# Attention and two mixture layers: the block-diagonal query tile written by ScalarE instead of copied by DMA

## Chip, cores and metric

The kernel runs on one core of a Trainium2 chip. A core has TensorE (PE in the profile; its weight loads are PEld), VectorE (DVE), ScalarE (ACT), GpSimd (POOL) and SyncE (SP, which issues the DMAs). The metric is the device time of one execution in microseconds; lower is better.

## The reference

Three steps follow each other; the change is in the first.

- Attention: q, k, v have shape (4, 8, 1152, 64), float32. Two neighbouring queries are averaged, which leaves 576 per head; then softmax(q_pool k^T / 8) v, with the row maximum subtracted before the exponential and 1e-9 added to the sum.
- A mixture of 8 experts over the 2304 tokens of 512 features: tokens are assigned greedily by sorted logits with a capacity of 288 each, then relu(x w1) w2.
- A dense layer: g = h - tanh(h) with h = x w_in, then g w_out.

## The kernel before, in words

Heads are handled two at a time, 16 pairs P = 0 to 15. The loop in `run` does the scores, exponentials and products with v of pair P; in between, a generator `prep(P + 1)` prepares the next pair. How far it advances is written out by hand: `SCHED` lists the steps (a step is half a score tile or a place behind pv) at which the generator is resumed, "B0" while pair 0 is worked on and "B" after that. Steps 2, 2 do the two query groups, 5, 5, 6 the three key groups, and the row-maximum matmuls begin at step 8 under "B" and at step 17 under "B0". In between stand the score matmuls (L227, L228) and their exponentials (E, L229) of the pair at work, and behind step 12 the pv matmuls (L245). Each engine works its instructions in the order written.

`prep` works in float32r, a rounded float32. For the queries: three transposes on TensorE put 288 columns of both heads into a PSUM buffer "aux" (L149; rows 0 to 63 are one head, 64 to 127 the other); ScalarE rounds it into qh (L152); VectorE stores the rest, ql = ps - qh (L153). The keys go the same way in three groups of 384 columns: L169, kh on ScalarE (L172), kl on VectorE (L173).

qz is a block-diagonal tile [128, 2, 576]: half s holds head s's rows of qh in that head's partitions, and zeros, set once at the start, in the other 64. It is the stationary operand of the row-maximum matmuls (L208): 9 blocks of 128 queries by 3 groups of 384 keys, each reduced on VectorE to a column of pm (L212). There is one qz for all pairs. In pair 0, VectorE and GpSimd fill it with casts from qh (L156); in the other 15 pairs two DMAs SBUF to SBUF do (L161), issued from SyncE's queue ahead of the six copies into q1 and q2 (L163 to L165). All these DMAs are shown under line 143, where the helper `copy` stands.

There are three PSUM buffers "aux". In a pair they are taken in turn by the two query groups, the three key groups and then the L208 products, and each comes free when VectorE has read it (ql, kl or pm). The score tiles have three buffers "sc" of their own. A product with v (`pv`) ends a pair; a copy oT on ScalarE (L252) starts the next. `finish(P)` does the row sums, normalisation and router logits of pair P during pair P + 1; at its very end, for the last pair, ScalarE reads one part of an aux buffer (L288) while VectorE reduces the rest of it (L290).

Of the kernel before, what the change touches and what calls it, by code (L numbers as in the profile page):

```python
# [14 lines left out]
AF = mybir.ActivationFunctionType  # L15
# [30 lines left out]
def as32(ap):  # L46
    return ap.bitcast(F32)


class Attention:  # L50
# [78 lines left out]
    def prep(self, P):  # L129
        nc, t = self.nc, self.t[P]  # L130
        first = P == 0
        bank = "sc" if first else "aux"
        qs, kr, qz = t["qs"], t["kr"], self.qz
        ql = self.wk.tile([128, SQ], F32R, name="ql", bufs=1)
        kh = self.wk.tile([128, S], F32R, name="kh", bufs=1)
        kl = self.wk.tile([128, S], F32R, name="kl", bufs=1)
        q1 = t["q1"] = self.wk.tile([128, 2, SQ], F32R, name="q1")
        q2 = t["q2"] = self.q2[P % 2]
        k1 = t["k1"] = [self.wk.tile([128, S], F32R, name=f"k1{s}") for s in range(2)]
        k2 = t["k2"] = [self.k2[2 * (P % 2) + s] for s in range(2)]  # L140
        own = [slice(0, 64), slice(64, 128)]
        oth = own[::-1]
        copy = lambda dst, src: nc.sync.dma_start(as32(dst), as32(src))

        qh = self.wk.tile([128, SQ], F32R, name="qh", bufs=1)
        for g in range(2):
            ps = self.psum.tile([128, 3, QP], F32, name="aux", bufs=3)
            for j in range(3):
                nc.tensor.transpose(ps[:, j], qs[:, 3 * g + j].rearrange("p s d -> p (s d)"), self.ident[:QP, :QP])  # L149
            ps = ps.rearrange("p a b -> p (a b)")  # L150
            c = slice(g * HALF, g * HALF + HALF)
            nc.scalar.activation(qh[:, c], ps, AF.Copy)  # L152
            nc.vector.tensor_sub(ql[:, c], ps, as32(qh[:, c]))  # L153
            if first:
                for s, e in ((0, nc.vector), (1, nc.gpsimd)):
                    e.tensor_copy(qz[own[s], s, c], qh[own[s], c])  # L156
                self.warm(4)
            yield
        if not first:
            for s in range(2):  # L160
                copy(qz[own[s], s], qh[own[s]])  # L161
        for s in range(2):
            copy(q1[own[s], s], qh[own[s]])  # L163
            copy(q1[oth[s], s], qh[own[s]])
            copy(q2[own[s], s], ql[own[s]])  # L165
        for g in range(3):
            ps = self.psum.tile([128, 3, 128], F32, name=bank, bufs=3)
            for j in range(3):
                nc.tensor.transpose(ps[:, j], kr[:, 3 * g + j].rearrange("p s d -> p (s d)"), self.ident)  # L169
            ps = ps.rearrange("p a b -> p (a b)")  # L170
            c = slice(g * 384, g * 384 + 384)
            nc.scalar.activation(kh[:, c], ps, AF.Copy)  # L172
            nc.vector.tensor_sub(kl[:, c], ps, as32(kh[:, c]))  # L173
            if first:
                self.warm(4)
            yield
        for s in range(2):
            copy(k1[s][own[s]], kh[own[s]])
            copy(k1[s][oth[s]], kl[own[s]])
            copy(k2[s][own[s]], kh[own[s]])  # L180
        qz = qz.rearrange("p s n -> p (s n)")
        pm = self.wk.tile([128, QB, 3], F32, name="pm")
        nm = self.wk.tile([128, QB], F32R, name="nm")

        def most(s):

            nb = slice(5 * s, 5 + 4 * s)
            nc.vector.tensor_reduce(nm[:, nb], pm[:, nb], axis=AX.X, op=OP.max, negate=True)
            yield
            yield  # L190
            at = 0
            for bs in ((range(4), range(4, 5)), (range(4, 5), range(5, 9)))[s]:
                ps = self.psum.tile([128, 512], F32, name="aux", bufs=3)
                n = 0
                for b in bs:
                    c = slice(0, 128) if b != 4 else own[s]
                    w = c.stop - c.start
                    nc.tensor.matmul(ps[:1, n:n + w], nm[:, b:b + 1], self.identr[:, c], start=True, stop=True)
                    n += w
                o = oth[s].start  # L200
                nc.scalar.activation(q2[o:o + 1, s, at:at + n], ps[:1, :n], AF.Copy)
                at += n
            yield

        for blk in range(QB):
            for pc in range(3):
                ps = self.psum.tile([128, 384], F32, name="aux", bufs=3)
                nc.tensor.matmul(ps, qz[:, blk * 128:blk * 128 + 128], kh[:, pc * 384:pc * 384 + 384],  # L208
                                 start=True, stop=True)
                if first and blk < 5:  # L210
                    self.warm(4)
                nc.vector.tensor_reduce(pm[:, blk, pc:pc + 1], ps, axis=AX.X, op=OP.max)  # L212
                yield
            if blk == 4:
                yield from most(0)
                if first:
                    yield "head"
        yield from most(1)
# [1073 lines left out]
```

## Time and profile before

| | |
|---|---|
| median of 3 runs | 1366.21 us (1364.76 to 1367.0) |
| the profiled execution | 1365.93 us |
| its span in the profile | 1364.1 us |
| TensorE busy | 1238.7 us (91%) |
| VectorE busy | 1050.1 us (77%) |
| ScalarE busy | 709.4 us (52%) |
| GpSimd busy | 571.2 us (42%) |

Times inside the profile are microseconds from the start of the span. A busy engine is not by itself a bound: what counts is which engine the others waited for at each place. The attention part covers about the first 600 us; a pair takes about 36 us.

### The profile page before, as it was taken

How to read it: one execution, taken by the hardware profiler on the slowest of the kernel's cores; microseconds unless marked ns; L12 is line 12 of the kernel's file. 1: busy time of each engine (PE TensorE's matmuls, PEld its weight loads, DVE VectorE, ACT ScalarE, POOL GpSimd, SP SyncE). 2: the span in 40 equal slices, each digit the busy share in tenths (PEclk: the TensorE clock that was granted, in tenths of full speed). 3: DMA queues.
4: the chain of work that ended last, by engine and by line, in shares of the span. 5: the costliest groups of instructions: out<-in, count | busy, mean ns of one | idle time of the engine just before them, and what ended most of it. 6: DMA issues, size and time to landing. Idle time of an engine off the chain costs nothing.

```text
span 1364.1 us, 26747 instructions
## 1 busy us (share of the span) xinstructions
PE 1238.7 (91%) x9539; PEld 1074.3 (79%) x9539; DVE 1050.1 (77%) x2384; ACT 709.4 (52%) x1892; POOL 571.2 (42%) x501
## 2 busy tenths in 40 slices
PE   7898888888988988866989999999999999999997
PEld 6666666666666666645879989899999999999997
DVE  6788888788878888886797888787877877557563
ACT  3554555555555555521455464653754645657464
POOL 5777777677667776520031221221312212222122
PEclk9999999999999999987999999999999999999999
DMA  8878878877777777325942402203114022040300
GB/s 195 217 199 207 210 205 206 209 185 180 189 204 195 202 198 195 120 67 161 323 135 72 120 17 74 79 9 101 51 33 120 17 88 65 17 135 18 95 1 18
DMA packets 164965, 175.01 MB, mean 128 GB/s; under 512 B 66400, under 2 KB 117600, under 8 KB 164832
## 3 DMA queue, kind: packets, MB, share of 16 engines
q1 hardware_dynamic: 161760, 163.86, 44.5%
q0 software_dynamic: 3072, 9.44, 2.4%
q8 instruction: 75, 1.23, 0.4%
q14 instruction: 58, 0.48, 0.1%
HBM read 100.16 MB, written 26.21 MB: 93 GB/s over the span
## 4 chain that ended last, share of the span: by engine, by line
PE 58%; DVE 29%; ACT 5%; DMA 3%; issue 3%; SPq 1%; POOL 1%; DVEq 0%; ACTq 0%; POOLq 0%
PE acc L908 19%; PE h L908 17%; PE pv L245 9%; DVE pm L212 8%; PE aux L208 4%; DVE db L789 3%; DMA qz<-qh 2%; DVE z L979 2%; PE sc L227 2%; DVE z L978 2%; DVE z L977 2%; PE sc L228 1%; DVE sm L290 1%; DVE sm L296 1%; PE aux L507 1%
## 5 line engine op out<-in xcount | busy, mean ns | idle before, releaser
L237 POOL TENSOR_TENSOR acc<-acc,E 128x576 f32<-128x576 f32 x217 | 327.3, 1522 | 106.2 <-ACT E L229 103.9
L229 ACT ACTIVATE E<-sc 128x288 f32<-128x288 f32 x576 | 224.9, 424 | 201.9 <-PE sc L228 119.7
L976 POOL TENSOR_TENSOR th<-hc,th 128x288 f32<-128x288 f32 x128 | 110.7, 865 | 383.2 <-ACT th L973 358.9
L212 DVE TENSOR_REDUCE pm<-aux 128x1 f32<-128x384 f32 x432 | 218.4, 548 | 50.1 <-PE aux L208 49.6
L908 PE MATMUL h<-yh,wi 128*128 128x288 f32 x1024 | 223.9, 300 | 3.5 <-ACT th L973 3.5
L208 PE MATMUL aux<-kh,qz 128*128 128x384 f32 x432 | 161.1, 383 | 31.5 <-DMA qz<-qh 8.9
L227 PE MATMUL sc<-q,k 128*128 128x288 f32 x576 | 183.1, 324 | 2.6 <-ACT E L229 2.3
L908 PEld LDWEIGHTS h<-yh,wi 128*128 128x128 f32 x1024 | 169.9, 189 | 5.1 <-ACT th L973 4.4
L228 PE MATMUL sc<-q,k 128*128 128x288 f32 x576 | 167.3, 295 | 0.0
L908 PE MATMUL acc<-ah,wo 128*128 128x288 f32 x1024 | 164.2, 299 | 0.0
L245 PE MATMUL pv<-E,vr 128*64 128x288 f32 x1152 | 154.0, 412 | 0.0
L908 PE MATMUL h<-yl,wi 128*128 128x288 f32 x512 | 147.4, 296 | 0.0
L908 PEld LDWEIGHTS acc<-ah,wo 128*128 128x128 f32 x1024 | 143.4, 188 | 3.1 <-issue 1.6
L208 PEld LDWEIGHTS aux<-kh,qz 128*128 128x128 f32 x432 | 79.4, 187 | 73.1 <-DVE pm L212 23.1
L227 PEld LDWEIGHTS sc<-q,k 128*128 128x128 f32 x576 | 109.2, 190 | 17.1 <-issue 8.3
L245 PEld LDWEIGHTS pv<-E,vr 128*64 128x64 f32 x1152 | 76.9, 136 | 56.1 <-issue 11.4
L977 DVE SCALAR_TENSOR_TENSOR z<-hc,z 128x288 f32<-128x288 f32 x128 | 63.5, 496 | 67.0 <-ACT mk L975 67.0
L228 PEld LDWEIGHTS sc<-q,k 128*128 128x128 f32 x576 | 109.3, 190 | 0.0
L971 ACT ACTIVATE z<-h 128x288 f32<-128x288 f32 x128 | 51.8, 405 | 89.7 <-PE h L908 89.6
L908 PEld LDWEIGHTS h<-yl,wi 128*128 128x128 f32 x512 | 95.4, 189 | 0.0
L908 PE MATMUL acc<-al,wo 128*128 128x288 f32 x512 | 88.9, 295 | 0.0
L979 DVE COPY_PREDICATED z<-mk,th 128x288 f32<-128x288 int16 x128 | 73.8, 576 | 13.6 <-DVE z L978 0.5
(246 smaller groups left out, 2481.6 us busy)
## 6 DMA issues: line engine op xcount, KB each, us to landing
k<-kh SPq DMA_DIRECT2D x64, 288.0 KB, 5.4
w1r<-in_moe_w_dram SPq DMA_DIRECT2D x64, 256.0 KB, 2.9
w2r<-in_moe_w_dram SPq DMA_DIRECT2D x64, 256.0 KB, 2.8
q<-qh SPq DMA_DIRECT2D x64, 144.0 KB, 2.6
k<-kl SPq DMA_DIRECT2D x32, 288.0 KB, 4.0
vr<-in_v_dram SPq DMA_DIRECT2D x16, 576.0 KB, 6.3
qr<-in_q_dram SPq DMA_DIRECT2D x30, 288.0 KB, 5.5
kr<-in_k_dram SPq DMA_DIRECT2D x30, 288.0 KB, 5.7
```

The costliest lines, as they stand in the source:

```text
L208: nc.tensor.matmul(ps, qz[:, blk * 128:blk * 128 + 128], kh[:, pc * 384:pc * 384 + 384], start=True, stop=True)
L212: nc.vector.tensor_reduce(pm[:, blk, pc:pc + 1], ps, axis=AX.X, op=OP.max)
L227: nc.tensor.matmul(ps, t["k1"][s][:, ks], t["q1"][:, s, qs], start=True, stop=False)
L228: nc.tensor.matmul(ps, t["k2"][s][:, ks], t["q2"][:, s, qs], start=False, stop=True)
L229: nc.scalar.activation(e[:, hf], ps, AF.Exp, scale=1.0 / 16.0)
L237: eng.tensor_add(a, a, e)
L245: nc.tensor.matmul(t["pv"][64 * s:64 * s + 64, hf, :HALF], t["vr"][:, s, c, :], t["E", c, s][:, hf], start=(c == 0), stop=(c == KC - 1), s ...
L908: self.nc.tensor.matmul(out, wl if p == 2 else wh, xl if p == 1 else xh, start=first and not seen[j], stop=last and seen[j] == 2)
L971: nc.scalar.activation(z, ps, AF.Square)
L976: nc.gpsimd.tensor_sub(th, h, th)
L977: nc.vector.scalar_tensor_tensor(z, h, LEAD, z, op0=OP.mult, op1=OP.mult)
L979: nc.vector.copy_predicated(z, mk.bitcast(mybir.dt.int16), th)
```

## The change

In `prep`, for every pair, ScalarE writes both halves of qz straight from the PSUM buffer, group by group, right behind qh and ahead of VectorE's subtraction in the program. The casts of the first pair and the two DMA copies of the other pairs go.

```diff
             nc.scalar.activation(qh[:, c], ps, AF.Copy)
+            for s in range(2):
+                nc.scalar.activation(qz[own[s], s, c], ps[own[s]], AF.Copy)
             nc.vector.tensor_sub(ql[:, c], ps, as32(qh[:, c]))
             if first:
-                for s, e in ((0, nc.vector), (1, nc.gpsimd)):
-                    e.tensor_copy(qz[own[s], s, c], qh[own[s], c])
                 self.warm(4)
             yield
-        if not first:
-            for s in range(2):
-                copy(qz[own[s], s], qh[own[s]])
```

## Rows read from the trace of the kernel before

**Rows 1.** Chain that ended last, shares of the span by line (page, part 4).

```profile
PE acc L908 19%; PE h L908 17%; PE pv L245 9%; DVE pm L212 8%; PE aux L208 4%; DVE db L789 3%; DMA qz<-qh 2%; DVE z L979 2%; PE sc L227 2%; DVE z L978 2%; DVE z L977 2%; PE sc L228 1%; DVE sm L290 1%; DVE sm L296 1%; PE aux L507 1%
```

**Rows 2.** Waits, 62 to 560 us: who <- whom: us in total, times, longest.

```profile
DVE kl L173 <- ACT kh L172: 10.8, 14, 0.8
...
PE aux L208 <- DMA qz<-qh: 8.9, 12, 1.3
...
PE aux L208 <- DVE kl L173: 1.6, 2, 1.1
```

**Rows 3.** Timeline, ScalarE, from 136 us: start us, us, instruction, [idle before].

```profile
136.33 0.74 ACT L152 ACTIVATE qh<-aux 128x288 fp32r<-128x288 f32 x2
136.91 1.06 ACT L229 ACTIVATE E<-sc 128x288 f32<-128x288 f32 x3
137.78 0.96 ACT L172 ACTIVATE kh<-aux 128x384 fp32r<-128x384 f32 x2
...
138.81 0.62 ACT L172 ACTIVATE kh<-aux 128x384 fp32r<-128x384 f32 x1
```

**Rows 4.** Timeline, VectorE, the same pair: first kl, all three, then pm.

```profile
138.39 0.56 DVE L173 TENSOR_TENSOR kl<-aux,kh 128x384 fp32r<-128x384 f32 x1 [0.78 <-ACT kh L172]
...
138.39 1.63 DVE L173 TENSOR_TENSOR kl<-aux,kh 128x384 fp32r<-128x384 f32 x3 [0.78 <-ACT kh L172]
140.04 2.42 DVE L212 TENSOR_REDUCE pm<-aux 128x1 f32<-128x384 f32 x5
...
144.27 0.56 DVE L212 TENSOR_REDUCE pm<-aux 128x1 f32<-128x384 f32 x1 [1.81 <-PE aux L208]
```

**Rows 5.** Timeline, TensorE, the same pair: L208, pv, a later L208.

```profile
139.59 0.41 PE L208 MATMUL aux<-kh,qz 128*128 128x384 f32 x1 [0.59 <-DMA qz<-qh]
...
140.99 0.33 PE L208 MATMUL aux<-kh,qz 128*128 128x384 f32 x1
...
141.43 0.34 PE L208 MATMUL aux<-kh,qz 128*128 128x384 f32 x1
141.69 0.71 PE L245 MATMUL pv<-E,vr 128*64 128x288 f32 x4
...
144.95 0.37 PE L208 MATMUL aux<-kh,qz 128*128 128x384 f32 x1
```

**Rows 6.** The copy in that pair: in the chain; in SyncE's timeline.

```profile
137.09 2.37 DMA qz<-qh
...
137.09 1.16 SPq L143 DMA_DIRECT2D qz<-qh  x2
```

**Rows 7.** ScalarE's groups by form, 62 to 560 us: busy us, mean ns, idle before.

```profile
L797 ACT ACTIVATE dh<-du 128x512 fp32r<-128x512 f32 x27 | 16.8, 622 | 17.6 <-DVE du L793 17.6
L201 ACT ACTIVATE q<-aux 1x512 fp32r<-1x512 f32 x28 | 16.4, 586 | 9.3 <-PE aux L198 9.3
```

**Rows 8.** Timelines at 598 us: two engines on one aux buffer.

```profile
598.59 0.19 ACT L288 ACTIVATION_READ_ACCUMULATOR xr<-aux 128x1 f32 x1
...
598.82 0.56 DVE L290 TENSOR_REDUCE sm<-aux 128x3 f32<-128x384 f32 x1
```

**Rows 9.** Pair 0's casts (min/median/max ns); pair 1's qs and its reader.

```profile
L156 DVE CAST qz<-qh x2: 872/990/1107, 8.7 to 10.1; 64x288 fp32r<-64x288 f32 x2
L156 POOL CAST qz<-qh x2: 422/422/423, 10.9 to 11.3; 64x288 fp32r<-64x288 f32 x2
...
29.02 1.79 POOL L127 TENSOR_TENSOR qs<-qr 96x768 f32<-96x768 f32 x1 [14.86 <-DMA qr<-in_q_dram]
...
30.87 0.47 PE L149 MATMUL aux<-ident,qs 96*128 96x96 f32 x3 [2.27 <-POOL qs L127]
```

**Rows 10.** Timelines of the pair at 31 us: VectorE and TensorE.

```profile
31.86 0.82 DVE L153 TENSOR_TENSOR ql<-aux,qh 128x288 fp32r<-128x288 f32 x2 [5.21 <-ACT qh L152]
...
31.98 1.94 PE L169 MATMUL aux<-ident,kr 128*128 128x128 f32 x9
```

**Rows 11.** Stretches: busy us of each engine, granted clock, DMA share, GB/s.

```profile
32.00:36.00 4.00, 4.00 (x21) 3.54 (x20) 2.82 (x6) 3.45 (x10) 3.77 (x4) 0.57 1.03 370
...
243.00:250.00 7.00, 5.69 (x44) 5.22 (x42) 4.21 (x11) 5.88 (x18) 3.19 (x3) 1.00 0.52 123
```

## Prediction, made before the changed kernel was run

> **What bounds the kernel now.** I read the chain that ended last first, then the waits, then the timeline of one pair of heads, engine by engine. In the chain [rows 1] the reader is to see that the attention part alternates between TensorE and VectorE (PE pv L245, DVE pm L212, PE aux L208), and that the copy "DMA qz<-qh" has 2% of it, some 27 us. That is the length of the copies on the chain, not what their removal gives back. What TensorE stood still for is in the waits [rows 2]: 14 pairs (those prepared under the schedule "B") begin their L208 matmuls after idle time, 12 times ended by the DMA and twice by VectorE's kl, 8.9 + 1.6 = 10.5 us in all. So at most 10.5 us hang on the DMA. The same rows show kl waiting for ScalarE's kh in all 14 pairs, 0.77 us each: next to the DMA, the path qs, kh (ScalarE), kl (VectorE), L208 is nearly as late.
>
> The pair at 136 us stands for the others. ScalarE is full: qh, qh, three E, kh, kh, E, kh follow each other without a gap [rows 3], and kh's first ends only then. The first kl ends at 138.39 + 0.56 = 138.95 and the last at 138.39 + 1.63 = 140.02 [rows 4]. The qz copy, issued at 137.09, lands 2.37 us later, 139.46 [rows 6], and the first L208 starts at 139.59 after 0.59 us of idle [rows 5]. Without the DMA it could start about 0.1 us behind the first kl, which frees its PSUM buffer (three "aux" buffers, taken by qs, qs, kr, kr, kr and then L208): 139.05. The slack the DMA takes is 0.5 us in such a pair.
>
> **The change, part by part.**
>
> *Four ACTIVATEs a pair are added*, two behind each qh, each 288 columns on 64 partitions. ScalarE starts a 288-column instruction every 0.29 us: (136.91 - 136.33) / 2 [rows 3]. No ScalarE row of this width has 64 partitions, so I bound it: one partition of 512 columns takes 586 ns and 128 partitions take 622 ns [rows 7]. Fewer partitions save at most 6%. I take 0.29 us, 4 x 0.29 = 1.16 us a pair, with ends of 4 x 0.27 = 1.09 us and 1.16 us. The Trainium skill, "ScalarE: Activation LUTs", section "What ACT_TABLE_LOAD costs", gives 186 ns + 0.833 ns a column with about 93 ns of overlap, as an estimate 0.33 us here; the rows of this kernel are faster, and by the page the sum below would be about 2.5 us larger.
>
> *What is queued behind them.* ScalarE works in order: three E and then kh stand behind the second qh. Nothing in that stretch is idle, so kh comes 1.16 us later, with its kl. In the pair at 136: first kl done 138.95 + 1.16 = 140.11, first L208 at about 140.2, against 139.59. The wait removed (0.5 us) is smaller than the push. Then the next buffers: the last kl ends at 140.02 + 1.16 = 141.18, and only behind it can VectorE start its reductions pm. The fourth L208 needs the first pm's buffer. A pm lasts 0.56 us and another starts every (2.42 - 0.56) / 4 = 0.47 us [rows 4]; an L208 that waits for a pm starts 0.12 us behind its end (144.95 against 144.27 + 0.56) [rows 4, 5]. So the first pm runs 141.20 to 141.76, the second to 142.22, and the fifth L208 starts at 142.34 against 141.43. The pv matmuls follow it by 0.26 us [rows 5]: 142.60 against 141.69, or +0.91 us. In before, pv does not wait for pm at this point, so the late kl turns into a pm wait as well.
>
> *Is it given back within the pair?* VectorE idles 1.81 us while pv runs [rows 4]; there the pushed pm fit without loss. But behind pv come L208 and pm again, each waiting for the other, to the pair's end, and I see no work outside this loop that would be waiting anyway. I carry the whole 0.91 us on.
>
> *The sum.* 14 x 0.91 = 12.7 us. Where the DMA landed later the loss is smaller by just that much: 10.5 us of idle is 10.5 - 14 x 0.59 = 2.2 us more than 14 typical pairs would have [rows 2, 5]. That leaves 10.5 us.
>
> *VectorE's subtraction ql now stands behind the two new reads of the same PSUM tile.* At the end of attention VectorE reduces three quarters of a buffer of which ScalarE reads the other; it starts at 598.82, right as ScalarE's instruction ends at 598.59 + 0.19 [rows 8], although neither uses what the other makes. So ql will start about 0.58 us later. The Trainium skill, "PSUM — Partial Sum Buffer", section "PSUM bank collisions raise a hardware error", says the same: two engines may not touch one bank and 32-partition quadrant at once, two reads included. In the 14 pairs this costs nothing, because the transposes of kr that wait for ql are ready for ScalarE long before kh's new turn; were kh not pushed, it would cost up to 0.3 us a pair.
>
> *The pair at 31 us* (schedule "B0", L208 ten steps later) has no such cover. Nine transposes of kr run one after another from 31.98 [rows 10], and the third group needs the second ql. That ql ends at 31.86 + 0.82 = 32.68; behind four copies it ends about 1.2 us later, near 33.9, and the third group, which began two thirds into that run, near 33.1, starts about 0.9 us later. Ends: 0 and 1.16 us; I take 0.9, as TensorE is the engine that everything follows there. By the reading in which VectorE may read beside ScalarE it would be about 0.3 us.
>
> *The first pair* loses two VectorE casts, one of 0.87 and one of 1.11 us, and two on GpSimd, of 0.42 us [rows 9]; ScalarE gets four copies. Its kl and pm come about 0.65 us sooner. This gives nothing: pair 1's qs waits for its load (14.86 us of idle ahead of it), and TensorE stands still 2.27 us behind that qs [rows 9]. Ends: -0.65 and 0.
>
> *Two DMA issues a pair go*, 1.16 us of SyncE's queue [rows 6]. The copies q<-qh behind them can start about 0.7 us sooner; their reader is the next pair's scores, some 30 us on. Nothing on the chain waits there, so 0; the earlier slot only matters if a load behind it were late.
>
> Together 10.5 + 0.9 = 11.4 us on the profiled execution's 1365.93 us: 1377.3, taken as 1377. The median of the runs is 1366.21, 0.3 us from that execution.
>
> **Rivals.**
>
> *Faster: the copies cost ScalarE next to nothing, and only the DMA wait goes.* For it: 12 of the 14 waits are put down to the DMA. Against it: kl is already late behind a full ScalarE [rows 2, 3]. With no push at all, pv would start at 140.02 + 0.02 + 0.56 + 0.47 + 0.12 + 0.26 = 141.45 against 141.69, a gain of 0.24 us, so 14 x 0.24 + 2.2 = 5.6 us, less 0.9 us in the pair at 31: 1361.2. It decides at a push of 4.7 / 14 = 0.34 us a pair, 0.08 us for one copy; the rows show 0.29.
>
> *Nothing: the push is real but is swallowed behind pv.* For it: VectorE's 1.81 us of idle and ScalarE's later gaps. Against it: the chain changes between PE and DVE without a third engine. 1366 to 1367.
>
> *TensorE's clock falls.* By the walk above TensorE's idle time between qh and pv grows from 0.59 to about 1.5 us a pair. After 2.27 us of stillness [rows 9] the granted clock was 0.57 over 32 to 36 us, between the two levels 1.2 and 2.4 GHz; around a stillness of 1.31 us in the 244 us pair it stayed 1.00 [rows 2, 11]. A stretch as at 32 us costs 4.0 x 0.43 = 1.7 us, over 14 pairs 24 us: 1401. Against it: the idle time comes in several pieces, for an E buffer, for kl and for pm, with matmuls between them.
>
> **How the numbers follow.** Forecast 0.79, faster rival 0.08, nothing 0.08, clock 0.05. The forecast's own range is 1371 to 1383: below, a push of 1.09 us, a third of the shift won back behind pv and nothing lost in the pair at 31 (14 x 0.84 x 2/3 - 2.2 = 5.6); above, no credit for the late DMAs and the pair at 31 at its end (14 x 0.91 + 1.16 = 13.9) and 3 us for changed overlaps of GpSimd and VectorE. The stated range, 1365.5 to 1383, takes in the case of nothing and leaves out the faster rival and the clock. A change under 0.2% (2.7 us) cannot be told from none here. Slower: 0.79 + 0.05 = 0.84, same 0.08, faster 0.08.
>
> **What would show it.** In the changed profile: four more ACT rows "qz<-aux" a pair, 0.29 us apart; ql about 0.58 us behind qh's end; the first kh about 1.16 us further from qh; "PE aux L208 <- DVE kl" in place of the DMA, with about as much idle or more; from the pair's first qh to its pv about 0.9 us more (5.36 us in the pair at 136), and the time from one pair to the next grown by the same. I am wrong if that distance is unchanged or shorter, if the pair's length doesn't follow it, or if L208 still starts where it did with kh pushed.

## The result, and the profile after

The changed kernel takes 1383.75 us (median of 4 runs, 1379.41 to 1388.45) against 1366.61 us before (1364.76 to 1367.19): ratio 1.0132, 95% interval 1.0113 to 1.0152. It is slower by 17 us; the prediction said 11, and 1383 at most. The profiled execution took 1384.49 us, with a span of 1382.7 us.

The waits of the 14 pairs come first (62 to 570 us; who <- whom: us in total, times, longest), against [rows 2]. Line numbers behind the edit are 3 lower: L208 is now L205, L173 is L170.

```profile
DVE ql L155 <- ACT qz L154: 38.9, 28, 4.1
...
PE sc L224 <- ACT E L226: 7.5, 14, 0.5
PE aux L166 <- DVE ql L155: 6.4, 14, 0.5
...
PE aux L205 <- DVE kl L170: 2.6, 14, 0.2
```

The DMA is gone, and with it the 10.5 us of idle ahead of L208. In its place TensorE waits 14 times each for a score buffer that E has yet to read, for ql and for kl (the last three rows, 16.5 us in all), and all three stand behind ScalarE.

ScalarE's timeline of the pair that began at 136 us before, with the second qz copy also shown by itself; to be read against [rows 3]:

```profile
138.89 0.43 ACT L152 ACTIVATE qh<-aux 128x288 fp32r<-128x288 f32 x1
139.18 0.41 ACT L154 ACTIVATE qz<-aux 64x288 fp32r<-64x288 f32 x1
...
139.60 0.41 ACT L154 ACTIVATE qz<-aux 64x288 fp32r<-64x288 f32 x1
...
140.03 0.41 ACT L152 ACTIVATE qh<-aux 128x288 fp32r<-128x288 f32 x1
140.34 0.81 ACT L154 ACTIVATE qz<-aux 64x288 fp32r<-64x288 f32 x2
141.17 1.02 ACT L226 ACTIVATE E<-sc 128x288 f32<-128x288 f32 x3
142.06 0.89 ACT L169 ACTIVATE kh<-aux 128x384 fp32r<-128x384 f32 x2
```

The first copy starts 0.29 us behind qh's start, while qh still runs. The second starts 0.42 us behind the first, at its end, and the second qh 0.43 us behind that, again at the end. So a group of qh and two copies takes 1.14 us instead of 0.29. kh starts 3.17 us behind qh (142.06 - 138.89), against 1.45 us before (137.78 - 136.33): a push of 1.72 us, where the prediction had 1.16.

VectorE and TensorE in the same pair, against [rows 4, 5]:

```profile
142.60 1.63 DVE L170 TENSOR_TENSOR kl<-aux,kh 128x384 fp32r<-128x384 f32 x3 [0.97 <-DMA q<-qh]
144.15 1.94 DVE L209 TENSOR_REDUCE pm<-aux 128x1 f32<-128x384 f32 x4
```

```profile
143.21 0.44 PE L205 MATMUL aux<-kh,qz 128*128 128x384 f32 x1 [0.18 <-DVE kl L170]
...
145.59 0.71 PE L242 MATMUL pv<-E,vr 128*64 128x288 f32 x4
```

From qh to pv it is 6.70 us (145.59 - 138.89), against 5.36 us. The label "DMA q<-qh" at kl is only the profile's guess at which of kl's waits ended last; kl starts as kh ends (142.06 + 0.51). What a whole pair takes is read from its first qh to that of another pair. Two rows of ScalarE's timeline of the kernel before, then two of the one after, 13 pairs apart:

```profile
63.91 0.43 ACT L152 ACTIVATE qh<-aux 128x288 fp32r<-128x288 f32 x1
...
532.36 0.43 ACT L152 ACTIVATE qh<-aux 128x288 fp32r<-128x288 f32 x1
```

```profile
64.55 0.43 ACT L152 ACTIVATE qh<-aux 128x288 fp32r<-128x288 f32 x1
...
548.01 0.43 ACT L152 ACTIVATE qh<-aux 128x288 fp32r<-128x288 f32 x1
```

A pair takes (548.01 - 64.55) / 13 = 37.19 us instead of 36.03, so 13 pairs lose 15.0 of the 18.6 us between the two profiled executions. The pair that began at 136 us itself grew from 35.81 to 37.14 us, by as much as its pv moved (1.34). Of the rest of the 18.6 us, 0.6 us lie ahead of 64 us and 3.0 us behind 548 us; those behind can't be put down to the change. From that last qh to the end of the span it takes 831.7 us before and 834.7 after, and 831.2 to 835.3 in the seven traces of the experiments, with 832.4 for the most delayed kernel of all (from qh) and 833.0 for the fastest (GpSimd).

### The profile page after: what moved, and what is told of

Same layout as the page of the kernel before. It is cut to its first block, busy times and chain, and to the rows that moved or that the text cites. A ratio compares the mean times of both kernels' runs of the same rounds, so it can differ in the third digit from the quotient of the medians.

```text
span 1382.7 us, 26720 instructions
## 1 busy us (share of the span) xinstructions
PE 1251.3 (90%) x9539; PEld 1078.6 (78%) x9539; DVE 1046.7 (76%) x2382; ACT 733.7 (53%) x1956; POOL 570.1 (41%) x499
## 4 chain that ended last, share of the span: by engine, by line
PE 57%; DVE 28%; ACT 7%; issue 3%; DMA 3%; SPq 1%; POOL 0%; DVEq 0%; ACTq 0%; POOLq 0%
PE acc L905 18%; PE h L905 16%; PE pv L242 9%; DVE pm L209 8%; PE aux L205 4%; DVE db L786 2%; DVE z L976 2%; PE sc L224 2%; DVE z L975 2%; ACT E L226 1%; DVE z L974 1%; PE sc L225 1%; DVE sm L287 1%; DMA q<-qh 1%; DVE sm L293 1%
## 5 line engine op out<-in xcount | busy, mean ns | idle before, releaser
L226 ACT ACTIVATE E<-sc 128x288 f32<-128x288 f32 x576 | 221.7, 417 | 195.1 <-PE sc L225 133.7
L209 DVE TENSOR_REDUCE pm<-aux 128x1 f32<-128x384 f32 x432 | 218.2, 547 | 43.8 <-PE aux L205 43.5
L205 PE MATMUL aux<-kh,qz 128*128 128x384 f32 x432 | 162.8, 387 | 22.6 <-DVE pm L209 6.2
L205 PEld LDWEIGHTS aux<-kh,qz 128*128 128x128 f32 x432 | 79.3, 187 | 64.5 <-DVE pm L209 21.8
```

The lines of the kernel that those rows point to most:

```text
L226: nc.scalar.activation(e[:, hf], ps, AF.Exp, scale=1.0 / 16.0)
```

## The experiments

Theory A: ScalarE's time between qh and kh sets the pair's start, and half-width copies hold it longer because the next instruction no longer starts before the last has ended. The rivals are VectorE's subtraction behind the copies (B) and the DMA wait alone (C). The "push" is how much further kh starts behind qh than before.

Four runs edit the changed kernel: full width, upper half first, grouped, and from qh. The other three (lower half alone, GpSimd, VectorE) edit the kernel before and leave its first pair as it was. Ratios are to the kernel before, which took 1365.77 us beside full width, lower half, from qh and GpSimd, and 1364.78 beside the rest.

**Copies of full width.** Each copy writes all 128 partitions. This overwrites the zeros of qz, so that the row maxima are those of both heads mixed; the instructions are otherwise the same.

```diff
-                nc.scalar.activation(qz[own[s], s, c], ps[own[s]], AF.Copy)
+                nc.scalar.activation(qz[:, s, c], ps, AF.Copy)
```

> The four copies a pair stay on ScalarE, but each writes all 128 partitions of its half of qz (so the zeros are overwritten and the row maxima are those of both heads mixed; the rest is unchanged). Theory A (the loss is the time that the copies hold ScalarE, and half-width copies hold it 0.43 us instead of 0.29 because the next instruction no longer starts before the last one ends): the copies start 0.29 us apart, kh comes 1.16 us later than before instead of 1.72, pv moves by about 0.8 us a pair instead of 1.34, and the time is about 1376 to 1378. Rival B (the loss is VectorE's subtraction standing behind the copies and holding the PSUM buffers): the same as the changed kernel, 1382 to 1386, since the subtraction stands behind them just the same.

Measured 1376.53 us, ratio to before 1.0078 (1.0060 to 1.0097). ScalarE's timeline, then TensorE's:

```profile
136.71 0.43 ACT L152 ACTIVATE qh<-aux 128x288 fp32r<-128x288 f32 x1
137.00 0.75 ACT L154 ACTIVATE qz<-aux 128x288 fp32r<-128x288 f32 x2
137.58 0.47 ACT L152 ACTIVATE qh<-aux 128x288 fp32r<-128x288 f32 x1
137.87 0.78 ACT L154 ACTIVATE qz<-aux 128x288 fp32r<-128x288 f32 x2
...
139.33 1.01 ACT L169 ACTIVATE kh<-aux 128x384 fp32r<-128x384 f32 x2
```

```profile
142.97 0.46 PE L242 MATMUL pv<-E,vr 128*64 128x288 f32 x2
```

Everything starts 0.29 us apart, twice as many lanes for less time, and kh stands 2.62 us behind qh: a push of 1.17 us. In this kernel pv comes 6.26 us behind qh (142.97 - 136.71), +0.90 us. That is the kernel that the prediction computed, to a microsecond (1377.3), though 0.9 us of that forecast were for a pair in which no loss shows. Rival B falls: TensorE's wait for ql is nearly the same here (5.3 us in 14 times, against 6.4), and 6 us of the loss are gone.

**The lower half alone on ScalarE**, the upper one by DMA as before.

```diff
+            if not first:
+                nc.scalar.activation(qz[own[0], 0, c], ps[own[0]], AF.Copy)
...
-            for s in range(2):
-                copy(qz[own[s], s], qh[own[s]])
+            copy(qz[own[1], 1], qh[own[1]])
```

> Only the lower half of qz (head 0, partitions 0 to 63) is copied by ScalarE, two copies a pair; the upper half stays a DMA, the first pair as before. The first reader, L208 blocks 0 to 3, needs the lower half alone. Two forms of theory A differ here. A1 (an instruction loses its early start when it leaves or enters the upper partitions, that is when the start partition changes): qh, copy and the next instruction start 0.29 us apart, the push is 0.58 us a pair and the time about 1368. A2 (any instruction behind a half-width one loses it): the next starts 0.43 us behind the copy, the push is 0.86 us and the time about 1372. Rival C (the wait for the DMA is what counts, copies are free): 1361.

Measured 1367.00 us, ratio 1.0011 (0.9998 to 1.0024): no change that can be told from none. A1 holds:

```profile
137.38 0.43 ACT L152 ACTIVATE qh<-aux 128x288 fp32r<-128x288 f32 x1
137.67 0.41 ACT L154 ACTIVATE qz<-aux 64x288 fp32r<-64x288 f32 x1
137.96 0.42 ACT L152 ACTIVATE qh<-aux 128x288 fp32r<-128x288 f32 x1
138.25 0.42 ACT L154 ACTIVATE qz<-aux 64x288 fp32r<-64x288 f32 x1
138.54 1.03 ACT L230 ACTIVATE E<-sc 128x288 f32<-128x288 f32 x3
```

Half-width instructions on partitions 0 to 63 keep the early start, 0.29 us each. It is not the width that costs. The wait for the DMA is gone here too (the first row-maximum matmul, now L209, starts 0.06 us behind the first kl), and the gain and the push of 0.58 us cancel: the mean pair is 36.06 us against 36.03. Rival C (1361) falls.

**The upper half first.** The loop runs over (1, 0) instead of (0, 1).

> The changed kernel with the upper half copied first, then the lower. A1a (every entry into and every exit from the upper partitions 64 to 127 costs the early start): qh 0.43 us to the upper copy's start, 0.42 to the lower's, 0.29 to the next instruction; kh 1.72 us later than before as in the changed kernel; 1381 to 1386. A1b (only going from the lower to the upper half and leaving the upper half cost it, going from all 128 partitions to the upper half does not): 0.29, 0.42, 0.29; kh 1.44 us later than before, about 1380.

Measured 1383.04 us, ratio 1.0134 (1.0099 to 1.0168), with the first three copies' starts:

```profile
139.02 0.43 ACT L152 ACTIVATE qh<-aux 128x288 fp32r<-128x288 f32 x1
139.47 0.41 ACT L154 ACTIVATE qz<-aux 64x288 fp32r<-64x288 f32 x1
...
139.89 0.40 ACT L154 ACTIVATE qz<-aux 64x288 fp32r<-64x288 f32 x1
...
140.19 0.39 ACT L152 ACTIVATE qh<-aux 128x288 fp32r<-128x288 f32 x1
140.61 0.82 ACT L154 ACTIVATE qz<-aux 64x288 fp32r<-64x288 f32 x2
```

0.45 and 0.42 into the upper copy, 0.42 from the upper to the lower, 0.30 from the lower to the next qh: A1a. Each entry into partitions 64 to 127 and each exit from them loses the early start; there are two a group in either order, and the time is that of the changed kernel.

**Grouped.** Lower halves behind each qh, both upper halves behind the second one.

```diff
+        held = []
...
-            for s in range(2):
-                nc.scalar.activation(qz[own[s], s, c], ps[own[s]], AF.Copy)
+            nc.scalar.activation(qz[own[0], 0, c], ps[own[0]], AF.Copy)
+            held.append((c, ps))
+            if g:
+                for c1, p1 in held:
+                    nc.scalar.activation(qz[own[1], 1, c1], p1[own[1]], AF.Copy)
```

> The same four copies, grouped: the lower half behind each qh, both upper halves behind the second qh's lower copy. A1 (the cost sits at the passage, not at the half): the two upper copies start 0.29 us apart, one passage in and one out instead of two of each, so kh comes 1.44 us later than before (1.16 + 2 x 0.14) and the time is about 1379 to 1381. Rival A3 (every copy of the upper half is slow by itself): the upper copies start 0.43 us apart and kh comes 1.6 to 1.72 us later, 1382 to 1385.

Measured 1379.26 us, ratio 1.0096 (1.0071 to 1.0121).

```profile
138.62 0.42 ACT L154 ACTIVATE qz<-aux 64x288 fp32r<-64x288 f32 x1
139.06 0.70 ACT L158 ACTIVATE qz<-aux 64x288 fp32r<-64x288 f32 x2
139.79 1.01 ACT L230 ACTIVATE E<-sc 128x288 f32<-128x288 f32 x3
```

Two upper copies together take 0.70 us, where 0.8 us is two without overlap: they do overlap, by about 0.1 us. The step into them (139.06 - 138.62 = 0.44) and the step out of them (139.79 is 0.03 us behind their end) are what is lost. Rival A3 falls; the cost sits at the passage, that is where an instruction on partitions 64 to 127 follows or precedes one that starts at partition 0. There are two of them a pair here instead of four, and kh comes 2.94 us behind qh, a push of 1.49 us.

**Copies from qh in SBUF**, so that ql needs not wait for them.

```diff
-                nc.scalar.activation(qz[own[s], s, c], ps[own[s]], AF.Copy)
+                nc.scalar.activation(qz[own[s], s, c], qh[own[s], c], AF.Copy)
```

> ScalarE's four half-width copies read qh in SBUF instead of the PSUM buffer, so VectorE's subtraction needs no longer wait for them. Theory A: ScalarE is held as long as in the changed kernel or longer (the first copy may have to wait for qh's end), kh is as late, and the time is 1382 to 1388. Rival B (the subtraction behind the copies holds the PSUM buffers, and TensorE's wait for it, 6.4 us in all, is part of the loss): 6 us less than the changed kernel, about 1377.

Measured 1391.85 us, ratio 1.0199 (1.0180 to 1.0217). ScalarE, VectorE, then a wait of TensorE (62 to 570 us):

```profile
141.72 0.43 ACT L152 ACTIVATE qh<-aux 128x288 fp32r<-128x288 f32 x1
142.18 0.90 ACT L154 ACTIVATE qz<-qh 64x288 fp32r<-64x288 f32 x2
143.10 0.41 ACT L152 ACTIVATE qh<-aux 128x288 fp32r<-128x288 f32 x1
```

```profile
142.18 0.46 DVE L155 TENSOR_TENSOR ql<-aux,qh 128x288 fp32r<-128x288 f32 x1 [1.34 <-ACT qh L152]
```

```profile
PE sc L224 <- ACT E L226: 23.5, 14, 1.7
```

ql starts at once, beside the copy, and the kernel is slower still: now the first copy waits for qh's end (142.18 - 141.72 = 0.46), and a group takes 1.38 us. kh is 3.63 us behind qh. TensorE no longer waits for ql, but 23.5 us for the score buffers behind ScalarE, where it was 7.5 in the changed kernel. B is out, and A goes further than the range that it gave (1388).

In all six kernels with copies on ScalarE the mean pair, read over 13 pairs as above, goes with the push: 0.58 us and 36.06 (lower half), 1.17 and 36.74 (full width), 1.49 and 36.95 (grouped), 1.72 and 37.19 (the changed kernel), 1.73 and 37.17 (upper half first), 2.18 and 37.77 (from qh).

**The casts on GpSimd**, from qh; ScalarE as before, no DMA.

```diff
+            else:
+                for s in range(2):
+                    nc.gpsimd.tensor_copy(qz[own[s], s, c], qh[own[s], c])
...
-        if not first:
-            for s in range(2):
-                copy(qz[own[s], s], qh[own[s]])
```

> GpSimd casts both halves from qh (four casts a pair, the first pair as before); no DMA for qz and nothing added on ScalarE. GpSimd stands idle for about 4 us at this place and a cast takes 0.42 us. Theory A (what ScalarE does between qh and kh sets the pair): kh comes as early as before, qz is ready about 1.7 us behind the first qh's end, ahead of the first kl, and the first L208 waits for kl alone: pv about 0.3 us earlier a pair and the late DMAs' 2.2 us saved, about 1360. Rival (the DMA wait hid something else that is late, such as the score tiles or the keys): no change, 1366. GpSimd slowed by VectorE: between the two.

Measured 1358.02 us (6 runs), ratio 0.9945 (0.9929 to 0.9962): faster than both, if by little. GpSimd, then TensorE:

```profile
137.02 1.87 POOL L160 CAST qz<-qh 64x288 fp32r<-64x288 f32 x4 [1.72 <-ACT qh L152]
139.39 1.45 POOL L234 TENSOR_TENSOR acc<-E,E 128x576 f32<-128x576 f32 x1 [0.49 <-ACT E L229]
```

```profile
139.29 0.41 PE L208 MATMUL aux<-kh,qz 128*128 128x384 f32 x1
...
141.57 0.71 PE L245 MATMUL pv<-E,vr 128*64 128x288 f32 x4
```

The four casts end at 138.89, ahead of the first kl (139.15), and fit where GpSimd stood idle anyway, with 0.49 us left. qh starts at 136.53 in this pair, so L208 follows it by 2.76 us (3.26 before) and pv by 5.04 (5.36 before).

**The copies on VectorE**, from PSUM, behind ql.

```diff
+            else:
+                for s in range(2):
+                    nc.vector.tensor_copy(qz[own[s], s, c], ps[own[s]])
...
-        if not first:
-            for s in range(2):
-                copy(qz[own[s], s], qh[own[s]])
```

> VectorE writes both halves of qz from the PSUM buffer, right behind its subtraction; ScalarE is as in the kernel before, no DMA for qz, first pair as before. Theory A asks what the copies push: four VectorE copies of about 0.4 us between ql and kl, where VectorE has 0.78 us free, so kl comes about 0.8 us later, pv about 0.4 us later than in the kernel before in a pair in which the DMA was on time, and the time is 1365 to 1371. Rival C (any engine is better than the DMA): 1358 to 1361 as with GpSimd.

Measured 1378.16 us, ratio 1.0088 (1.0062 to 1.0113): outside the range that I gave. VectorE, ScalarE, then a wait of TensorE (62 to 570 us):

```profile
141.29 0.46 DVE L153 TENSOR_TENSOR ql<-aux,qh 128x288 fp32r<-128x288 f32 x1 [1.34 <-ACT qh L152]
141.66 0.91 DVE L160 CAST qz<-aux 64x288 fp32r<-64x288 f32 x2
142.61 0.46 DVE L153 TENSOR_TENSOR ql<-aux,qh 128x288 fp32r<-128x288 f32 x1
142.98 0.91 DVE L160 CAST qz<-aux 64x288 fp32r<-64x288 f32 x2
143.93 1.02 DVE L173 TENSOR_TENSOR kl<-aux,kh 128x384 fp32r<-128x384 f32 x2
```

```profile
142.27 0.58 ACT L172 ACTIVATE kh<-aux 128x384 fp32r<-128x384 f32 x1
143.28 0.49 ACT L172 ACTIVATE kh<-aux 128x384 fp32r<-128x384 f32 x1 [0.43 <-PE aux L169]
```

```profile
PE aux L169 <- DVE qz L160: 17.2, 28, 0.7
```

A group takes 1.32 us (142.61 - 141.29), 0.95 us of it for two copies, where I had counted some 0.4 us a copy. qh starts at 140.82 in this pair, so kl comes 3.11 us behind it, 1.05 later than before, where I had 0.8. The copies also hold the PSUM buffers, so that the transposes of kr wait for them (17.2 us in 28 times) and ScalarE with the transposes (0.43 us): one late chain feeds another, and the mean pair is 36.72 us, 0.68 more than before. That makes some 9.5 of the 13.4 us. In the profiled execution another 2.9 us lie in the pair at 31 us, where the granted clock was 0.77 over 28 to 50 us (0.92 before); whether the copies have to do with that is not shown. C, any engine but the DMA, is wrong here too.

## Why the prediction was wrong

The direction and the mechanism were right, a term was mis-sized. By its steps:

- *"Four ACTIVATEs a pair are added", "I take 0.29 us, 4 x 0.29 = 1.16 us a pair".* This step failed. The four took 1.72 us, since two passages of some 0.14 us a group came on top: 0.29, 0.42 and 0.43 in place of three times 0.29. Both ends, 1.09 and 1.16, were taken from the price of few against many partitions [rows 7], and that price is right (the lower half alone: 0.29). What I did not bound was where the partitions lie. With copies of full width the push is 1.17 us and the loss 10.8 us; with half-width copies it is 17.1. The 6.4 us between them are the miss (17.1 against 11.4), and a little more: 0.9 us that were forecast elsewhere did not come.
- *The walk from the push to pv, +0.91 us.* At the push that it assumed it held: +0.90 with full width. By the walk pv moves by the push less 0.25 us; at 1.72 us that is 1.47, and pv moved by 1.34.
- *Nothing is given back within the pair.* Right: pv later by 1.34 us, and the pairs longer by 1.16 us on average, since the late DMAs of some pairs no longer count. The rival "swallowed behind pv" falls.
- *The subtraction behind the copies costs nothing in the 14 pairs.* Right. ql did start behind the copies (0.7 us behind qh's end, as the second copy went slower), TensorE waited 6.4 us for it in all, but only in time that it would have spent waiting for ScalarE: with ql free, the loss is as large for its push (3.63 - 1.45 = 2.18 us; by the sum of the prediction 14 x 1.93 - 2.2 = 24.8 us, measured 26.1).
- *The pair at 31 us, +0.9.* Not seen: from its first qh to the next pair's it took 32.49 us before (63.91 - 31.42) and 32.20 after (64.55 - 32.35); in the other four kernels with all four copies on ScalarE it is 32.2 to 32.5. Taking that term out, the prediction with the shift of pv as measured would be 14 x 1.34 - 2.2 = 16.6 us, against 17.1 measured.
- *"PE aux L208 <- DVE kl" in place of the DMA, with about as much idle or more.* The wait came, but with 2.6 us in place of 10.5. TensorE had stood still earlier in the pair, for ql and for the score buffers, and so reached this matmul late itself. The two waits that [rows 2] put down to kl were the DMA's as well: in both pairs the first kl had ended at least 0.6 us ahead of L208. The 10.5 us are right all the same.
- *First pair, DMA issues, clock.* No gain or loss shows that can be told from the scatter of the executions. The granted clock was 1.00 over 62 to 570 us, the full level, with all the waits above; that rival did not happen.
- *The faster rival* named the right wait and the wrong engine: it had 1361.2 with no push at all, and GpSimd, which gives none, reached 1358.0.

What stays open: why the four runs of the changed kernel spread over 9 us. The mean granted clock goes with it, 0.985 in the fastest and 0.980 in the slowest. In the profiled one the clock was 0.77 over 615 to 695 us, behind the attention, against 0.84 over 600 to 680 us before; why it differs is not shown.

## What to carry to other kernels

A DMA on the chain is worth only what it is later than the next chain; here that was 0.5 us of 2.4. Before work is moved to an engine, look at what stands behind it in that engine's order at that place, not at its share of busy time: ScalarE had 52%, and no gap between qh and kh, while GpSimd had the room. Price an instruction by a row with the same partitions, start included; where there is none, leave room above for the lost overlap.

## What was not expected of the hardware

On ScalarE an instruction of 288 columns starts 0.29 us behind the one ahead of it, before that one's end (0.43 us). Where one works on partitions 64 to 127 and its neighbour starts at partition 0, this is lost: 0.40 to 0.45 us, in both directions, whether the neighbour covers 64 or 128 partitions. Two on 64 to 127 in a row keep it (0.31 us). VectorE shows a like step: 0.37 us from ql to the lower copy, then 0.95 us from there to the next ql over both copies, where twice 0.37 would be about 0.75; no run changed the order there. Other start partitions were not tried, nor copies that read one half and write the other.

The trace of before had what may be a hint of it. ScalarE's 1-partition copies q (L201) write partition 0 or 64. At 131.81 one writes partition 0, and the next instruction starts ahead of its end (131.81 + 0.59); at 154.38 two write partition 64, and the next starts behind their end (154.38 + 0.69):

```profile
131.81 0.59 ACT L201 ACTIVATE q<-aux 1x512 fp32r<-1x512 f32 x1 [0.45 <-PE aux L198]
132.31 0.61 ACT L797 ACTIVATE dh<-du 128x512 fp32r<-128x512 f32 x1
...
154.38 0.69 ACT L201 ACTIVATE q<-aux 1x512 fp32r<-1x512 f32 x2 [0.21 <-PE aux L198]
155.10 0.41 ACT L229 ACTIVATE E<-sc 128x288 f32<-128x288 f32 x1
```

It fits the same step, but isn't shown to be it: these copies read partition 0 and only write partition 64, and the score tile could have come late.
